# A second softmax with its maximum subtracted on TensorE, two blocks that alternate two steps earlier, and a weight decode whose low bits come a step later

## The chip, the cores and the metric

The kernel runs on one core of a Trainium2 chip. The metric is the time of one execution on the device in microseconds (us), lower is better. Before the change the median of three runs is 979.04 us (977.61 to 979.51).

## The reference, cut to what matters

Three stages follow one another. An attention over 4 batches, 8 heads, 576 positions, 64 columns per head, with a local mask for the first four heads (32 positions back) and a strided one for the others; then a feed-forward layer with `h * cos(h)`; then one with a rational function of h.

```
scores = where(mask, scale * q @ k.T, -1e9);  scores -= max(scores)
attn = exp(scores);  attn /= sum(attn) + 1e-9;  x = attn @ v      # heads side by side: 2304 x 512
x = g(x @ w_in) @ w_out        # 512 -> 2048 -> 512, g(h) = h * cos(h)
out = g2(x @ w_in2) @ w_out2   # g2(h) = P(h) / Q(h)
```

## The kernel before, in words

Five engines run their own queues, strictly in the order in which the program issues to them: PE (TensorE), DVE (VectorE), ACT (ScalarE), POOL (GpSimd) and SP, which issues the DMAs. The order is written out by hand; an instruction that waits holds up all that stands behind it on its engine.

*Attention.* The work is cut into eight halves of a sequence, n = 0 to 7 (288 positions each), and each half into four pairs of heads, pr = 0 to 3 (0 and 1 local, 2 and 3 strided). For half 1 a pair has 5 blocks of queries: 445 score columns for pr 0 and 1 in one bank of PSUM, 378 + 252 = 630 for pr 2 and 3 in two banks. For each pair: `att_s` puts mask and scores into PSUM, the softmax follows, `att_norm` divides by the sum (two small DVE instructions and a multiplication on POOL), `att_t`, `att_te` and `att_o` transpose, copy and multiply with v, and `att_oe` writes the result as a high part `xh` (ACT, L374) and a low part `xl` (DVE, L375) into a ring that the feed-forward layer reads.

*START* is a list of commands that handles half 0, and of half 1 the scores and the exponentials, beside the decoding of the first eight weight tiles. `red` takes row maxima on DVE (L292) and scales them (L293). `exps` issues five activations per pair, one for each block, each with the negative maximum as its bias and its row sum accumulated on the side (L302).

*Steps.* After START come steps g = 0, 1, 2, ... A step is one block of tokens with one of 16 slices f of the hidden layer: `l1` has 12 matmuls (L408), the elementwise part follows, and `l2` (12 matmuls, L427) comes two or three steps later. The element-wise part of a step is a string of letters, in whose order the engines get their instructions: U (ACT, L497), V (DVE, L507), N (ACT sine, L509), M (DVE, L511), G (ACT, L515), H (POOL or DVE, L517), `x y z p q` for weight decoding, `s w` for splits, `T` for the attention's PE part, `L` for what is planned as "late". In the first 32 steps M reads h from PSUM, and `l1` has two banks for h, so that `l1` of step g waits for M of step g - 2. Two blocks of 256 tokens, bA and bB, share the first 32 steps: bA alone for `BLAG` steps, then in turns. bB reads columns 256 to 511 of the ring, which are partly of half 1. `TAB1` says in which steps the rest of half 1 runs (norm, transposes, result).

*Weights.* They come as 64-bit integers and are decoded in place. For each 128 x 512 tile: two activations (L143 for the value, L147 for the low bits), two DVE instructions (`c == 1`, L154, which reads the low bits, and `c == 2`, L156; `c == 0` does nothing), then a split into high (ACT, L162) and low part (POOL, L165). `DSTEP` gives the step in which pair k = 4 to 15 of tiles of the first layer is decoded; the ACT part runs at the end of the step ahead of it, the split in the step behind it. The second layer's tiles are decoded in steps 28 to 111 by `plan_w2`, with `first` (ACT part), `second` with c = 0 and c = 1, and `third`, in steps that `W2ABS` gives, most often with c = 0 and c = 1 in the same step, the one behind `first`.

Of the kernel before, what the change touches and what calls it, by code (L numbers as in the profile page):

```python
# [73 lines left out]


ORD.update({0: 'LukjVsWxyzNMabpqTGH', 1: 'UjVLwxyzNMpTbsaGqH', 2: 'UjVTxwKyNMbsazpqGHL', 3: 'UKjVbTwxLyzNaMsqGHp', 4: 'UjVaTwxyzNMLbpsqGH', 5: 'UjVsTxyzNMpwabqGHL', 6: 'UKxjVwyszbTNMaGpqHL', 7: 'ULKjVTwxyzNMabpqGsH', 8: 'uajVTswxyzbNMpqGHL', 9: 'ULjVTswxyzqpNMabGH', 10: 'sUxWyjVbKzNMpqGHTLa', 11: 'UjVswxzNyMabpqGTHL', 12: 'uKxjVwyszbTNMaGpqHL', 13: 'TUjVsxyzwLNabpMqGH', 14: 'uKwbSTxjVyzNMaLqpGH', 15: 'UKxJVyTswzNMbqpaLGH', 16: 'UajVKsxyNzpTwMGbqHL', 17: 'UajVKsxyNzMpTwGbqHL', 18: 'bUKjVswxyTzNLMapqGh', 19: 'UjVTxwKyNMLsbazpqGH', 20: 'UwxyJVbKzNMpqsGhTLa', 21: 'UKjVbTwxLyzNaMsqGHp', 22: 'uxTswyzMapGbjVqNHL', 23: 'uTxswzyMapGbjVqNhL', 24: 'ujVaswxyzNMkbpqGHLT', 25: 'UxTsWyzMapGbJVqKNHL', 26: 'sUMNTWxyzpabqGHKjVL', 27: 'uTWxzbsNMjVaqypGHKL', 28: 'NMUjVTkGhswL', 29: 'wNsMUjVGTLhk', 30: 'UxjVswyTbzkNMaGpqHL', 31: 'ULKjVTswxyzqpNMabGH', 32: 'UjVswxyTbzKNMaGpqHL', 33: 'bUKjVswxyTzNLMapqGh', 34: 'swNMUjVGhTL', 35: 'skwNMLUGTjVh', 36: 'sNMwLUkGhTjV', 37: 'wNTMuKjVLSGH', 38: 'skwNMLUGTjVh', 39: 'SwKNMujVGHTL', 40: 'SwNMUKjVGHTL', 41: 'swNMUKjVGHTL', 42: 'swNMUKjVGHTL', 43: 'wNTMuKjVLSGH', 44: 'swNMUKjVGhTL', 45: 'swNMUKjVGhTL', 46: 'swNMUKjVGHTL', 47: 'swNMUKjVGHTL', 112: 'swNMUKjVGHTL', 113: 'swNMUKjVGhTL', 114: 'swNMUKjVGhTL', 115: 'swNMUKjVGhTL', 116: 'swNMUKjVGHTL', 117: 'swNMUKjVGhTL', 118: 'swNMUKjVGhTL', 119: 'swNMukjVGHTL', 120: 'swNMUKjVGHTL', 121: 'swNMUKjVGHTL', 122: 'swNMUKjVGhTL', 123: 'swNMUKjVGhTL', 124: 'swNMUKjVGhTL', 125: 'swNMUKjVGhTL', 126: 'swNMUjKVGHTL', 127: 'swNMUKjVGHTL'})
DSTEP = [0, 1, 2, 3, 4, 6, 5, 8, 10, 12, 14, 15]
TAB1 = [[0, 2, 3], [0, 3, 4], [3, 4, 5], [4, 5, 6]]
TAB2 = [[-3, -1, -1, 0, 6, 8, 11], [-3, 1, -2, 1, 6, 10, 12], [-3, 12, 2, 3, 6, 11, 13], [2, 11, 4, 5, 8, 12, 14]]
W2ABS = [[25, 28, 29, 30, 31], [34, 37, 38, 38, 38], [37, 40, 41, 41, 42], [41, 44, 45, 45, 46], [48, 51, 52, 52, 52], [52, 55, 56, 56, 57], [57, 60, 61, 62, 63], [64, 67, 68, 68, 68], [68, 71, 72, 72, 73], [73, 76, 77, 78, 79], [80, 83, 84, 84, 84], [84, 87, 88, 88, 89], [89, 92, 93, 94, 95], [96, 99, 100, 100, 100], [100, 103, 104, 104, 105], [105, 108, 109, 110, 111]]  # L80
BLAG = 8
START = ['cst ACT', 'lq 0 0', 'lq 0 2 ACT', 'load 2 0', 'lv 0 1', 'lv 0 3 w0', 'lq 0 3', 'lq 0 1 ACT', 'load 0 0', 'lv 0 0', 'load 0 1', 'load 1 0 ACT', 'load 1 1', 'warm 38', 'lv 0 2 w0', 'masks', 's 0 0 y', 's 0 1 y', 's 0 2 y', 's 0 3 y', 'lq 1 0', 'ab', 'lq 1 2', 'lq 1 1', 'load 2 1', 'load 3 0', 'load 3 1', 'red 0 0', 'lv 1 0', 'exps 0 0', 'lq 1 3', 'ms 0 1', 'ex 0 1', 'red 0 2', 'lv 1 1', 'exps 0 2', 'norm 0 0 POOL', 'ms 0 3', 'ex 0 3', 'load 4 1', 'sum 0 1', 'norm 0 2 POOL', 'norm 0 1 POOL', 'sum 0 3', 'warm 29', 'abs 0 0', 'abs 0 1', 't 0 0 h', 'load 4 0', 'te 0 0', 'd 0 0 0', 'norm 0 3 POOL', 'o 0 0', 'd 0 1 0', 'd 0 0 1', 'd 0 1 1', 'd 0 0 2', 'd 0 1 2', 't 0 1 y', 'abs 1 1', 'te 0 1', 'oe 0 0', 'split 0 1 POOL', 'abs 1 0', 't 0 2 h', 'o 0 1', 'd 1 1 0', 'd 1 1 1', 'd 1 0 0', 'te 0 2', 'load 6 1', 'd 1 0 1', 'split 0 0 POOL', 'd 1 0 2', 't 0 3 y', 'oe 0 1', 's 1 0 y', 'te 0 3', 'd 1 1 2', 'o 0 2', 'split 1 0 POOL', 'oe 0 2', 'split 1 1 POOL', 'o 0 3', 's 1 1 y', 'abs 2 0', 'abs 2 1 DVE', 'd 2 0 0', 'd 2 1 0', 'abs 3 0', 'd 2 0 1', 'd 2 1 1', 'abs 3 1', 's 1 2 y', 's 1 3 a', 'red 1 0', 'd 2 1 2', 'red 1 1', 'd 2 0 2', 'exps 1 0', 'oe 0 3', 'split 2 0 POOL', 'exps 1 1', 'red 1 2', 'split 2 1 POOL', 'd 3 1 0', 'red 1 3', 'exps 1 2', 'exps 1 3', 'd 3 0 0', 'd 3 0 1', 'd 3 1 1', 'd 3 0 2', 'd 3 1 2', 'split 3 0 POOL', 'load 5 0', 'load 5 1', 'load 7 0', 'split 3 1 POOL DVE', 'load 7 1', 'load 6 0', 'next']
LV1 = [2, 4]
TABE = [[-5, -2, -1, 0, 4, 9, 11], [-3, -1, 0, 1, 6, 10, 12], [0, 12, 2, 3, 6, 11, 13], [1, 13, 4, 5, 6, 12, 14]]
TABO = [[-4, -2, -1, 0, 4, 9, 11], [-3, -1, 0, 1, 6, 10, 12], [-2, 12, 2, 3, 4, 11, 13], [1, 13, 4, 5, 6, 12, 14]]
C_ORD.update({0: 'swNMUKjVGHTL', 1: 'swNMUjVGhTL', 2: 'swNMUKjVGhTL', 3: 'swNMUKjVGhTL', 4: 'swNMUKjVGhTL', 5: 'swNMUKjVGhTL', 6: 'swNMUKjVGhTL', 7: 'swNMUkjVGHTL', 8: 'swNMUKjVGHTL', 9: 'swNMUKjVGHTL', 10: 'swNMUKJVGhTL', 11: 'swNMUKjVGhTL', 12: 'swNMUKjVGhTL', 13: 'swNMUKjVGhTL', 14: 'swNMUKjVGHTL', 15: 'swNMUKjVGHTL', 16: 'swNMUKjVGHTL', 17: 'swNMUKjVGhTL', 18: 'swNMUKjVGhTL', 19: 'swNMUKjVGhTL', 20: 'swNMUKjVGHTL', 21: 'swNMUKjVGhTL', 22: 'swNMUKjVGhTL', 23: 'swNMUjVGhTL', 24: 'swNLMUKjVGHT', 25: 'wNsMUKjVGHTL', 26: 'swNMUKjVGhTL', 27: 'swNMUKjVGhTL', 28: 'swNMUKjVGhTL', 29: 'swNMUKjVGhTL', 30: 'swNMUKjVGHTL', 31: 'swNMUKjVGHTL'})
# [5 lines left out]
def attention_moe_moe_kernel(ctx: ExitStack, tc: tile.TileContext, qk0, qk, vv, w1, w2, consts, a, b, out):  # L92
    nc = tc.nc
    ACT, DVE, POOL, PE, SP = nc.scalar, nc.vector, nc.gpsimd, nc.tensor, nc.sync
# [11 lines left out]
    cst = const.tile([128, NCONST], F32, name="cst")  # L106
# [3 lines left out]
    ab = const.tile([128, 6], F32, name="ab")  # L110
# [17 lines left out]
    wh, wl, raws = {}, {}, {}  # L128
# [6 lines left out]
        (eng or SP).dma_start(out=t.rearrange("p n w -> p (n w)"), in_=src[f, o].bitcast(I32))  # L135
        raws[key, f, o] = t

    def dec_abs(key, f, o, eng=None):
        t = raws.pop((key, f, o))
        m = stage("dec")  # L140
        src = t[:, :, 1].bitcast(F32)
        if eng is None:
            ACT.activation(out=m, in_=src, func=AF.Copy, scale=2.0 ** -112)  # L143
        else:
            eng.tensor_scalar(out=m, in0=src, scalar1=2.0 ** -112, scalar2=None, op0=ALU.mult)

# [577 lines left out]
    for k in range(NPRE, NF):  # L724
        dplan[DSTEP[k - NPRE]] = pairs[k]
    with tc.manual_schedule():
        with tc.tile_pool(name="att", bufs=2) as p:
# [6 lines left out]
            ms = {}  # L734
# [182 lines left out]
```

## Time and profile before

| | |
|---|---|
| median of three runs | 979.04 us |
| the profiled execution: time, and span from first to last instruction | 975.9 us, 974.1 us |
| PE busy | 919.2 us, 94% of the span |
| DVE, ACT, POOL busy | 700.5, 707.9, 292.5 us |
| mean granted clock of TensorE | 0.987 |

Times within the execution count from the first instruction. "V of step g" below is the g-th instruction of line L507 (counted from 0); it marks when DVE has come to step g.

### The profile page before, as it was taken

The page shows a single profiled execution, that of the slowest core. Times are in us where ns is not written, and L with a number is a line of the kernel's source. Part 1 is how long each engine was busy: PE and PEld are TensorE (multiplying, and loading weights), DVE is VectorE, ACT ScalarE, POOL GpSimd, SP SyncE. Part 2 cuts the span into 40 slices and gives each one's busy share as a digit, 9 for nine tenths or more (in the row PEclk, how much of TensorE's full clock was granted, in tenths as well). Part 3 has the DMA queues.
Part 4 walks back from the last instruction along what each step waited for, and adds up shares of the span by engine and source line. Part 5 has one row for each costly group of instructions (what it writes and reads, how often), then busy time and mean ns, then how long its engine had stood idle before and what let it go on. Part 6 is the DMA issues. An engine that isn't in the chain of part 4 may idle for free.

```text
span 974.1 us, 17268 instructions
## 1 busy us (share of the span) xinstructions
PE 919.2 (94%) x6367; PEld 857.1 (88%) x6367; DVE 700.5 (72%) x1305; ACT 707.9 (73%) x1485; POOL 292.5 (30%) x279
## 2 busy tenths in 40 slices
PE   7678999999999999999899999999999999999997
PEld 6567999998989989899899978888898898898895
DVE  5997754775555575656658797787787787787776
ACT  5987765665775865757758877777777877777875
POOL 2577722142222132221312223223223223232221
PEclk9799999999999999999999999999999999999999
DMA  9766104435335244344226420010100100100000
GB/s 309 265 221 210 45 2 129 152 112 149 114 101 156 93 144 140 130 136 148 91 78 201 128 78 1 8 58 1 40 26 1 66 1 1 66 1 0 34 1 33
DMA packets 51525, 89.35 MB, mean 92 GB/s; under 512 B 4584, under 2 KB 28400, under 8 KB 51440
## 3 DMA queue, kind: packets, MB, share of 16 engines
q1 hardware_dynamic: 50720, 86.58, 27.0%
q10 hardware_dynamic: 720, 1.67, 0.5%
q8 instruction: 50, 0.82, 0.3%
q14 instruction: 35, 0.29, 0.1%
HBM read 70.40 MB, written 17.83 MB: 91 GB/s over the span
## 4 chain that ended last, share of the span: by engine, by line
PE 23%; ACT 22%; DVE 19%; POOL 10%; issue 5%; DMA 1%; POOLq 0%; ACTq 0%; DVEq 0%
PE h L408 10%; POOL z L467 9%; PE y L427 9%; DVE r L470 7%; ACT r L466 6%; ACT r L465 5%; ACT gh L476 4%; DVE h L471 3%; DVE a L471 3%; PE a L363 1%; PE a L248 1%; DVE t L511 1%; PE a L344 1%; ACT dec L143 1%; ACT L509 1%
## 5 line engine op out<-in xcount | busy, mean ns | idle before, releaser
L408 PE MATMUL h<-xh,w 128*128 128x288 f32 (+3 forms) x1408 | 338.6, 312 | 15.5 <-DVE t L511 11.9
L408 PEld LDWEIGHTS h<-xh,w 128*128 128x128 f32 x1408 | 245.1, 191 | 21.7 <-DVE t L511 13.1
L427 PE MATMUL y<-gh,w 128*128 128x288 f32 (+2 forms) x1024 | 229.3, 300 | 0.5 <-ACT w L162 0.5
L408 PE MATMUL h<-xl,w 128*128 128x288 f32 (+3 forms) x704 | 206.8, 310 | 0.0
L427 PE MATMUL y<-w,gh 128*128 128x512 f32 x576 | 195.9, 393 | 5.6 <-DVE ev L441 4.6
L467 POOL TENSOR_TENSOR z<-q,r 128x384 f32<-128x384 f32 x96 | 97.4, 1014 | 297.9 <-ACT r L466 287.8
L427 PEld LDWEIGHTS y<-gh,w 128*128 128x128 f32 x1024 | 172.1, 189 | 0.8 <-ACT w L162 0.8
L427 PE MATMUL y<-gl,w 128*128 128x288 f32 (+2 forms) x512 | 151.7, 296 | 2.2 <-POOL gl L517 2.1
L408 PEld LDWEIGHTS h<-xl,w 128*128 128x128 f32 x704 | 134.7, 191 | 1.8
L427 PEld LDWEIGHTS y<-w,gh 128*128 128x128 f32 x576 | 108.1, 188 | 28.1 <-DVE ev L441 7.1
L517 POOL TENSOR_TENSOR gl<-t,gh 128x288 fp32r<-128x288 f32 (+2 forms) x67 | 68.6, 1025 | 186.9 <-ACT gh L515 162.0
L470 DVE SCALAR_TENSOR_TENSOR r<-z,r 128x384 f32<-128x384 f32 x96 | 69.5, 724 | 74.1 <-POOL z L467 74.1
L427 PE MATMUL y<-w,gl 128*128 128x512 f32 x288 | 114.7, 398 | 5.2 <-DVE gl L481 5.0
L497 ACT ACTIVATE t<-h,biases 128x288 int32<-128x288 f32 (+2 forms) x116 | 57.7, 497 | 78.5 <-PE h L408 66.1
L507 DVE SCALAR_TENSOR_TENSOR u<-h,t 128x288 f32<-128x288 f32 (+2 forms) x128 | 58.2, 455 | 68.5 <-ACT hs L503 53.3
L408 PE MATMUL a<-xh,w 128*128 128x384 f32 x384 | 106.2, 337 | 0.0
L427 PEld LDWEIGHTS y<-gl,w 128*128 128x128 f32 x512 | 97.1, 190 | 3.0 <-POOL gl L517 2.9
L515 ACT ACTIVATE gh<-t 128x288 fp32r<-128x288 f32 (+2 forms) x128 | 56.7, 443 | 27.7 <-DVE t L511 25.6
L509 ACT ACTIVATE u<-u,biases 128x288 f32<-128x288 f32 (+2 forms) x128 | 67.8, 530 | 12.1 <-DVE u L507 11.7
L511 DVE TENSOR_TENSOR t<-u,hs 128x288 f32<-128x288 f32 (+1 forms) x91 | 49.2, 541 | 36.7 <-ACT u L509 36.5
L408 PEld LDWEIGHTS a<-xh,w 128*128 128x128 f32 x384 | 70.5, 188 | 1.8
L427 PEld LDWEIGHTS y<-w,gl 128*128 128x128 f32 x288 | 54.0, 188 | 20.1 <-DVE gl L481 12.1
(113 smaller groups left out, 1612.9 us busy)
## 6 DMA issues: line engine op xcount, KB each, us to landing
raw<-in_w_dram SPq DMA_DIRECT2D x63, 512.0 KB
qk<-in_qk_dram SPq DMA_DIRECT2D x18, 481.0 KB
wf<-dec SPq DMA_DIRECT2D x32, 256.0 KB
wf<-wf SPq DMA_DIRECT2D x32, 256.0 KB
x2s<-x2d SPq DMA_DIRECT2D x24, 192.0 KB
out_dram<-ev SPq DMA_DIRECT2D x17, 256.0 KB
v<-in_vv_dram SPq DMA_DIRECT2D x16, 240.0 KB
v<-in_vv_dram SPq DMA_DIRECT2D x24, 157.5 KB
```

Of the source, the lines that this page charges most:

```text
L408: PE.matmul(h[:, :n], w[d["ph"], f, 0][:, 128 * c:128 * c + 128], x[c][:, cs], start=k == 0, stop=k == len(ops) - 1)
L427: PE.matmul(y, l, r, start=first and i == 0 and bk != bB, stop=last and i == 2 and bk != bA)
L466: ACT.activation(out=r, in_=r, func=AF.Exp, scale=-1.0, bias=biases[:, 1:2])
L467: POOL.tensor_tensor(out=z, in0=q, in1=r, op=ALU.mult)
L470: DVE.scalar_tensor_tensor(out=r, in0=z, scalar=2.0, in1=r, op0=ALU.subtract, op1=ALU.mult, reverse0=True)
L471: DVE.scalar_tensor_tensor(out=h, in0=h, scalar=ab[:, 0:1], in1=r, op0=ALU.add, op1=ALU.mult)
L497: ACT.activation(out=k, in_=h, func=AF.Identity, scale=INV_2PI, bias=biases[:, 2:3])
L507: DVE.scalar_tensor_tensor(out=u, in0=h, scalar=INV_2PI, in1=k, op0=ALU.mult, op1=ALU.subtract)
L509: ACT.activation(out=u, in_=u, func=AF.Sin, scale=TWO_PI, bias=biases[:, 3:4])
L511: DVE.tensor_tensor(out=t, in0=u, in1=e.get("hs", h), op=ALU.mult)
L515: ACT.activation(out=e["gh"], in_=t, func=AF.Copy)
L517: (POOL if c == "H" else DVE).tensor_tensor(out=e["gl"], in0=t, in1=e["gh"].bitcast(F32), op=ALU.subtract)
```

## The change

Half 1's softmax in START: `red`, `exps` become `redn` (the same reductions, the maximum only negated), `psub`, `ex`, `sum`. `psub` is `att_s` a second time on the same banks: mask and scores anew, and behind them one float32 matmul of the identity with the negative maxima, broadcast over the columns. `ex` is one activation for each bank (one for pr 0 and 1, two for pr 2 and 3) instead of five with sums, and `sum` a reduction on DVE over the pair. `oe 0 3` moves ahead of half 1's reductions. `BLAG` goes from 8 to 6; `TAB1` moves half 1's steps one to two earlier; the loads of v for half 1 go to steps 1 and 2; `DSTEP` moves pairs 8, 10, 11 and all later ones one to three steps back, and 9 stays at step 6. For the second layer's weights the low-bits activations move from `first` to `second` with c = 0.

```diff
-DSTEP = [0, 1, 2, 3, 4, 6, 5, 8, 10, 12, 14, 15]
-TAB1 = [[0, 2, 3], [0, 3, 4], [3, 4, 5], [4, 5, 6]]
+DSTEP = [0, 1, 2, 3, 5, 6, 8, 10, 12, 14, 16, 18]
+TAB1 = [[0, 1, 2], [0, 2, 3], [1, 3, 4], [2, 4, 5]]
-BLAG = 8
+BLAG = 6
-START = [... 's 1 2 y', 's 1 3 a', 'red 1 0', 'd 2 1 2', 'red 1 1', 'd 2 0 2', 'exps 1 0', 'oe 0 3', 'split 2 0 POOL', 'exps 1 1', 'red 1 2', 'split 2 1 POOL', 'd 3 1 0', 'red 1 3', 'exps 1 2', 'exps 1 3', 'd 3 0 0', 'd 3 0 1', 'd 3 1 1', 'd 3 0 2', 'd 3 1 2', 'split 3 0 POOL', ..., 'split 3 1 POOL DVE', ..., 'next']
-LV1 = [2, 4]
+START = [... 's 1 2 y', 's 1 3 a', 'oe 0 3', 'redn 1 0', 'psub 1 0', 'd 2 1 2', 'redn 1 1', 'psub 1 1', 'd 2 0 2', 'ex 1 0', 'sum 1 0', 'split 2 0 POOL', 'ex 1 1', 'sum 1 1', 'redn 1 2', 'psub 1 2', 'split 2 1 POOL', 'd 3 1 0', 'redn 1 3', 'psub 1 3', 'ex 1 2', 'sum 1 2', 'ex 1 3', 'sum 1 3', 'd 3 0 0', 'd 3 0 1', 'd 3 1 1', 'd 3 0 2', 'd 3 1 2', 'split 3 0 POOL', ..., 'split 3 1 POOL DVE', ..., 'next']
+LV1 = [1, 2]
...
+    def dec_low(t):
+        src = t.rearrange("p n w -> p (n w)").bitcast(U8).rearrange("p (n b) -> p n b", b=8)[:, :, 3]
+        ACT.activation(out=t[:, :, 0], in_=src, func=AF.Copy, scale=1.0 / 32.0, bias=-31.0 / 64.0)
-    def dec_abs(key, f, o, eng=None):
+    def dec_abs(key, f, o, eng=None, low=True):
...
             def first(f=f):
-                raws["m", f] = [dec_abs(2, f, o) for o in range(2)]
+                raws["m", f] = [dec_abs(2, f, o, low=False) for o in range(2)]
             def second(f=f, c=0):
                 for t, m in raws["m", f]:
-                    dec_ops(c, t, m)
+                    dec_ops(c, t, m) if c else dec_low(t)
```

## Rows read from the trace of the kernel before

**Rows 1.** The page's busy time, share of the span and instructions of each engine.

```profile
PE 919.2 (94%) x6367; PEld 857.1 (88%) x6367; DVE 700.5 (72%) x1305; ACT 707.9 (73%) x1485; POOL 292.5 (30%) x279
```

**Rows 2.** Windows: start and end, length, busy time of each engine, clock, DMA.

```profile
29.43:39.21 9.78, 6.78 (x45) 5.77 (x45) 9.22 (x20) 9.78 (x47) 2.62 (x3) 0.65 1.02 392
31.00:37.80 6.80, 4.72 (x28) 3.99 (x25) 6.30 (x13) 6.80 (x37) 2.54 (x2) 0.50 1.03 410
42.25:93.46 51.21, 37.15 (x311) 34.67 (x312) 44.50 (x62) 42.41 (x90) 37.67 (x30) 0.88 0.61 208
127.62:142.02 14.40, 14.40 (x122) 14.31 (x121) 7.03 (x19) 10.01 (x18) 3.08 (x4) 1.00 0.00 1
```

**Rows 3.** PE's waits, first 200 us, then the rest: total, times, longest.

```profile
PE h L408 <- DVE t L511: 7.6, 2, 5.8
...
PE h L408 <- DVE t L511: 4.3, 2, 2.2
```

**Rows 4.** Timeline of ACT, end of START and step 0: start, duration, instruction.

```profile
30.28 0.34 ACT L302 ACTIVATE p<-y,mx 128x89 f32<-128x89 f32 x1
...
31.85 0.68 ACT L374 ACTIVATE xh<-a 128x288 fp32r<-128x288 f32 x1
...
38.81 0.79 ACT L143 ACTIVATE dec<-raw 128x512 f32<-128x512 f32 x1
...
41.27 1.28 ACT L509 ACT_TABLE_LOAD   x1
42.70 0.51 ACT L509 ACTIVATE u<-u,biases 128x256 f32<-128x256 f32 x1 [0.15 <-DVE u L507]
```

**Rows 5.** Timeline of DVE, from half 1's first reduction to V of step 10.

```profile
29.43 0.61 DVE L292 TENSOR_REDUCE mx<-y 128x5 f32<-128x445 f32 x1
...
32.56 0.65 DVE L375 TENSOR_TENSOR xl<-a,xh 128x288 fp32r<-128x288 f32 x1 [0.39 <-ACT xh L374]
33.12 0.87 DVE L292 TENSOR_REDUCE mx<-y 128x3 f32<-128x378 f32 x2
...
36.35 1.28 DVE L154 SCALAR_TENSOR_TENSOR dec<-dec,raw 128x512 int32<-128x512 int32 x2
37.55 1.28 DVE L156 SCALAR_TENSOR_TENSOR dec<-raw,dec 128x512 int32<-128x512 int32 x2
...
39.21 1.25 DVE L333 TENSOR_SCALAR sm<-sm 128x5 f32<-128x5 f32 x1
...
42.25 0.42 DVE L507 SCALAR_TENSOR_TENSOR u<-h,t 128x256 f32<-128x256 f32 x1
...
63.51 0.42 DVE L507 SCALAR_TENSOR_TENSOR u<-h,t 128x256 f32<-128x256 f32 x1 [0.64 <-ACT t L497]
...
93.46 0.42 DVE L507 SCALAR_TENSOR_TENSOR u<-h,t 128x256 f32<-128x256 f32 x1 [0.98 <-ACT t L497]
```

**Rows 6.** Timeline of PE: masks and scores of half 1 (pr 0, 2, 3).

```profile
21.46 0.35 PE L237 MATMUL y<-msk,cst 128*128 128x445 bf16 x1
21.75 0.98 PE L245 MATMUL y<-qk 64*64 64x89 f32 x20
...
27.81 0.65 PE L245 MATMUL y<-k,qk 64*64 64x126 f32 x8
...
33.59 1.10 PE L245 MATMUL a<-k,qk 64*64 64x126 f32 x8
```

**Rows 7.** Groups by line and shape, whole span: count, busy us, mean ns of one.

```profile
L286 DVE TENSOR_REDUCE sm<-p 128x5 f32<-128x445 f32 x13 | 7.9, 606 | 0.0
...
L281 ACT ACTIVATE p<-p 128x445 f32<-128x445 f32 x13 | 7.4, 577 | 1.8 <-DVE p L315 1.7
...
L286 DVE TENSOR_REDUCE sm<-p 128x5 f32<-128x630 f32 x6 | 4.8, 800 | 0.0
```

**Rows 8.** Timeline around a decoding step of the second layer's weights (steps 55 to 57).

```profile
272.72 0.64 ACT L147 ACTIVATE raw<-raw 128x512 int32<-128x512 uint8 x1
...
273.40 0.69 DVE L154 SCALAR_TENSOR_TENSOR dec<-dec,raw 128x512 int32<-128x512 int32 x1 [0.40 <-ACT raw L147]
274.00 0.45 DVE L511 TENSOR_TENSOR t<-u,h 128x288 f32<-128x288 f32 x1
...
274.50 0.40 PE L408 MATMUL h<-xh,w 128*128 128x288 f32 x1 [2.19 <-DVE t L511]
```

More of the change, by code (lines that the diff above doesn't have):

```diff
@@ L82 @@
-START = ['cst ACT', 'lq 0 0', 'lq 0 2 ACT', 'load 2 0', 'lv 0 1', 'lv 0 3 w0', 'lq 0 3', 'lq 0 1 ACT', 'load 0 0', 'lv 0 0', 'load 0 1', 'load 1 0 ACT', 'load 1 1', 'warm 38', 'lv 0 2 w0', 'masks', 's 0 0 y', 's 0 1 y', 's 0 2 y', 's 0 3 y', 'lq 1 0', 'ab', 'lq 1 2', 'lq 1 1', 'load 2 1', 'load 3 0', 'load 3 1', 'red 0 0', 'lv 1 0', 'exps 0 0', 'lq 1 3', 'ms 0 1', 'ex 0 1', 'red 0 2', 'lv 1 1', 'exps 0 2', 'norm 0 0 POOL', 'ms 0 3', 'ex 0 3', 'load 4 1', 'sum 0 1', 'norm 0 2 POOL', 'norm 0 1 POOL', 'sum 0 3', 'warm 29', 'abs 0 0', 'abs 0 1', 't 0 0 h', 'load 4 0', 'te 0 0', 'd 0 0 0', 'norm 0 3 POOL', 'o 0 0', 'd 0 1 0', 'd 0 0 1', 'd 0 1 1', 'd 0 0 2', 'd 0 1 2', 't 0 1 y', 'abs 1 1', 'te 0 1', 'oe 0 0', 'split 0 1 POOL', 'abs 1 0', 't 0 2 h', 'o 0 1', 'd 1 1 0', 'd 1 1 1', 'd 1 0 0', 'te 0 2', 'load 6 1', 'd 1 0 1', 'split 0 0 POOL', 'd 1 0 2', 't 0 3 y', 'oe 0 1', 's 1 0 y', 'te 0 3', 'd 1 1 2', 'o 0 2', 'split 1 0 POOL', 'oe 0 2', 'split 1 1 POOL', 'o 0 3', 's 1 1 y', 'abs 2 0', 'abs 2 1 DVE', 'd 2 0 0', 'd 2 1 0', 'abs 3 0', 'd 2 0 1', 'd 2 1 1', 'abs 3 1', 's 1 2 y', 's 1 3 a', 'red 1 0', 'd 2 1 2', 'red 1 1', 'd 2 0 2', 'exps 1 0', 'oe 0 3', 'split 2 0 POOL', 'exps 1 1', 'red 1 2', 'split 2 1 POOL', 'd 3 1 0', 'red 1 3', 'exps 1 2', 'exps 1 3', 'd 3 0 0', 'd 3 0 1', 'd 3 1 1', 'd 3 0 2', 'd 3 1 2', 'split 3 0 POOL', 'load 5 0', 'load 5 1', 'load 7 0', 'split 3 1 POOL DVE', 'load 7 1', 'load 6 0', 'next']
@@ L83 @@
-LV1 = [2, 4]
+BLAG = 6
+START = ['cst ACT', 'lq 0 0', 'lq 0 2 ACT', 'load 2 0', 'lv 0 1', 'lv 0 3 w0', 'lq 0 3', 'lq 0 1 ACT', 'load 0 0', 'lv 0 0', 'load 0 1', 'load 1 0 ACT', 'load 1 1', 'warm 38', 'lv 0 2 w0', 'masks', 's 0 0 y', 's 0 1 y', 's 0 2 y', 's 0 3 y', 'lq 1 0', 'ab', 'lq 1 2', 'lq 1 1', 'load 2 1', 'load 3 0', 'load 3 1', 'red 0 0', 'lv 1 0', 'exps 0 0', 'lq 1 3', 'ms 0 1', 'ex 0 1', 'red 0 2', 'lv 1 1', 'exps 0 2', 'norm 0 0 POOL', 'ms 0 3', 'ex 0 3', 'load 4 1', 'sum 0 1', 'norm 0 2 POOL', 'norm 0 1 POOL', 'sum 0 3', 'warm 29', 'abs 0 0', 'abs 0 1', 't 0 0 h', 'load 4 0', 'te 0 0', 'd 0 0 0', 'norm 0 3 POOL', 'o 0 0', 'd 0 1 0', 'd 0 0 1', 'd 0 1 1', 'd 0 0 2', 'd 0 1 2', 't 0 1 y', 'abs 1 1', 'te 0 1', 'oe 0 0', 'split 0 1 POOL', 'abs 1 0', 't 0 2 h', 'o 0 1', 'd 1 1 0', 'd 1 1 1', 'd 1 0 0', 'te 0 2', 'load 6 1', 'd 1 0 1', 'split 0 0 POOL', 'd 1 0 2', 't 0 3 y', 'oe 0 1', 's 1 0 y', 'te 0 3', 'd 1 1 2', 'o 0 2', 'split 1 0 POOL', 'oe 0 2', 'split 1 1 POOL', 'o 0 3', 's 1 1 y', 'abs 2 0', 'abs 2 1 DVE', 'd 2 0 0', 'd 2 1 0', 'abs 3 0', 'd 2 0 1', 'd 2 1 1', 'abs 3 1', 's 1 2 y', 's 1 3 a', 'oe 0 3', 'redn 1 0', 'psub 1 0', 'd 2 1 2', 'redn 1 1', 'psub 1 1', 'd 2 0 2', 'ex 1 0', 'sum 1 0', 'split 2 0 POOL', 'ex 1 1', 'sum 1 1', 'redn 1 2', 'psub 1 2', 'split 2 1 POOL', 'd 3 1 0', 'redn 1 3', 'psub 1 3', 'ex 1 2', 'sum 1 2', 'ex 1 3', 'sum 1 3', 'd 3 0 0', 'd 3 0 1', 'd 3 1 1', 'd 3 0 2', 'd 3 1 2', 'split 3 0 POOL', 'load 5 0', 'load 5 1', 'load 7 0', 'split 3 1 POOL DVE', 'load 7 1', 'load 6 0', 'next']
@@ L145, in dec_abs @@
             eng.tensor_scalar(out=m, in0=src, scalar1=2.0 ** -112, scalar2=None, op0=ALU.mult)
-        ACT.activation(out=t[:, :, 0], in_=t.rearrange("p n w -> p (n w)").bitcast(U8).rearrange("p (n b) -> p n b", b=8)[:, :, 3],
-                       func=AF.Copy, scale=1.0 / 32.0, bias=-31.0 / 64.0)
+        if low:
+            dec_low(t)
         return t, m
```

## The prediction

> **What bounds the kernel now.** The page's busy times come first: PE is busy for 94% of the span, the other engines for at most 73% [rows 1]. So an edit pays or costs where PE waits, and the windows tell where that is. In a stretch such as 127.62 to 142.02 us PE is busy for all 14.40 us, 122 matmuls or about five steps, 2.9 us for each, and DVE and ACT have room [rows 2]. From 42.25 to 93.46 us, which is V of step 0 to V of step 10, it is busy for 37.2 of 51.2 us, while DVE is busy for 44.5, ACT for 42.4 and POOL for 37.7 [rows 2]: these ten steps take 5.1 us each, not 2.9, because three engines are busy with decoding, half 1's attention and the elementwise part at once. Ahead of that, 29.43 to 39.21 us, the end of START, ACT is busy for 9.78 of 9.78 us and DVE for 9.22 [rows 2]. The waits of PE say the same: its longest, 5.8 us, is `l1` waiting for M (L511), early on; in the remaining 774 us the same wait occurs twice, 4.3 us in all [rows 3]. The reader is to see two clocks in the timeline: DVE comes to step 0 at 42.25 us and ACT's sine (N) at 42.70 us [rows 4, 5], and PE is the bound from about 93.5 us on. The change counts for what it does to these two, and for the two late waits.
>
> **START, the chain that gets longer.** Before, the four `exps` stand in ACT's queue between 30.28 us and 38.2 us, ACT goes on with step 0's decode at 38.81, loads the sine's table at 41.27, and N starts at 42.70 [rows 4]. DVE does its reductions and four decode instructions (36.35 to 38.83), then two norms, whose L333 takes 1.25 us [rows 5]. The two engines hardly wait for each other. After, every pair goes DVE (`redn`), PE (`psub`), ACT (`ex`), DVE (`sum`), and DVE's order puts `sum` 0 and 1 ahead of `redn` 2 and 3, and all `sum`s ahead of the decode of the tiles that ACT needs next. I follow it by hand:
>
> `oe 0 3` goes first: `xh` starts at 30.28 and not at 31.85 [rows 4], `xl` (0.65 us) [rows 5] ends about 31.6, and the last scores, which ended at 34.69 [rows 6], end 1.57 earlier, at 33.1. The first `redn` (0.61 and a short negation) is done at 32.3, in time. Then `psub`. Its masks and scores are those of before: 1.27 us from the first mask to the last score for a pair with 445 columns [rows 6]; for one with 630, 252 of which take 0.65 [rows 6], some 1.9 with masks. The broadcast matmul isn't in the trace. From below: 445 columns of bf16 in one matmul take 0.35 us [rows 6]; from above: ten pairs of float32 matmuls of 89 columns take 0.98 us, 0.49 for 445 columns [rows 6]. I take 0.42, as it is float32 but without ten starts, and 0.6 for 630. A `psub` is then 1.7 us, or 2.5.
>
> - pair 0: PE 33.1 to 34.8; `ex` (0.58) [rows 7] to 35.4; `sum` (0.61) [rows 7] to 36.1
> - pair 1: PE to 36.5; `ex` to 37.1, `sum` to 37.8
> - `redn` of pair 2 (0.87 [rows 5] and the negation) to 38.8, of pair 3 to 39.9; PE starts pair 2 under the reduction and ends it at 40.8, pair 3 at 43.2
> - `ex` of pair 3's second bank to 43.7; `sum` (0.80) [rows 7] to 44.5
> - the four decode instructions, 2.5 us [rows 5], to 47.0 instead of 38.83
>
> So DVE is some 8.2 us late. Of that 2.8 us are the four `sum`s (2 x 0.61 and 2 x 0.80), the rest waits for PE and ACT. Behind it stand the norms, which still meet POOL's splits, and V of step 0. On ACT the split's copy waits for the decode, then come four activations of `next` (38.81 to about 41.0 before) and the table: N of step 0 also about 8.3 us later, near 51.0. What `ex` saves on ACT, 20 activations with sums against six (about 6.5 us against 2.5), is worth nothing here, since ACT now waits for `psub`.
>
> That is at full clock. Between 31.00 and 37.80 the granted clock was 0.50 [rows 2], after PE had stood waiting at the end of START; at that level scores like those of 0.65 us take 1.10 [rows 6], 1.7 times as long. With all four `psub`s at the lower level the same chain ends 14.3 us late. PE waits less now just ahead of the first `psub`, so I take mostly the upper level, and 9.5 us (8.3 to 14.3).
>
> The Trainium skill, page "FP8 and Floating Point Precision", section "TensorE Precision Notes", has a true float32 product in four passes through the array. An estimate by that page, four passes at 2.4 GHz, would be 0.74 us for 445 columns and 1.05 for 630, and START some 1.5 us longer than I sum it, +6.5 us in all. The rows speak against it, as 445 columns of float32 scores fit into 0.49 us [rows 6]; no row here shows a single long float32 matmul.
>
> **Steps 0 to 9, where something comes back.** `DSTEP` takes one pair out of these steps: eight are decoded there before (steps 0 to 6 and 8), seven after (0, 1, 2, 3, 5, 6, 8). `TAB1` moves half 1's transposes from steps 2 to 5 to steps 1 to 4 and its norms forward. Before, V of step 4 is at 63.51 [rows 5]: 21.3 us for four steps with decode, then 29.95 us for six steps with four decodes. After, the first four have the same decodes and one pair's transposes, copies and results more, +1.5 us by the 0.65 of `xl` and the like. The six that follow have three decodes and three steps free of one. At the average decode step of 5.3 us (21.3 / 4), less 0.4 as the attention is done after step 5, and 3.4 for a free step, they take 25.0 where 29.95 stood. That is 3.5 us back. The other end is that PE becomes the bound from step 6 on, at 2.9 us a step [rows 2]: 9.5 us back. I take 5. The two sides add: V of step 10 comes 9.5 - 5 = 4.5 us later, and from there on PE bounds both kernels.
>
> **BLAG, LV1, later decodes.** Alternating from step 6 changes no matmul count. `l1` of step 6 needs half 1's last `xl` of step 5, one step ahead where two were; DVE issues it right at the start of step 5, whose predecessor has no decode, so at most 0.6 us, within the range. Each weight is still ready two steps ahead of its matmul (pair 8 is split in step 6, used by `l2` in step 9). The loads of v stand in SP's queue behind the multiplication that frees their buffer, one step ahead of their use; at 5 us a step I take nothing. Decodes in steps 16 and 18 lie beside half 2's maxima on DVE and POOL: up to 1 us.
>
> **Low bits.** Two activations of 0.64 us [rows 8] move one step. Before step 57 PE waits 2.19 us [rows 8], one of the two late waits [rows 3]; there M (274.00) stands behind the low bits of `first` on ACT and, in that step's order, behind L154, which ends at 274.09. After, ACT's sine comes 1.1 us earlier, but the low bits follow it and both L154 wait for them, ahead of M: M moves from 274.00 to about 274.45. So +0.45 us, twice; or, if M should profit, up to 4.3 us back [rows 3]. I take +0.5. In other steps ACT's peak falls by 1.1 us under PE's cover.
>
> **Sum.** 9.5 - 5.0 + 0.5 = +5.0 us on the profiled 975.9, that is 980.9. The profiled execution is 3.1 us under the median, so the forecast for a median is 979.0 + 5.0 = 984.0 us, 0.5% slower. About 0.2%, 2 us, is what a measurement can tell from no change.
>
> **Rivals.**
> - *The clock falls in START:* PE waits for `redn` between `psub` 1 and 2, and the lower level holds for pairs 2 and 3, or all: +12 to +14 in START, some 4 to 5 back, +7 to +10: 986 to 989. For it: 0.50 was granted in this very place [rows 2]. Against: more matmuls. Chance 0.18.
> - *Even:* START costs 8.3 to 9.5 and the steps give 8 back, 977 to 981. For it: PE's 2.9 us from step 6 on is what the steps behind 93 us show. Against: three decodes are still in steps 5 to 8. Chance 0.18.
> - *Faster:* the first ten steps are freed of more than they are given. Place: steps 4 to 9. It decides when these six steps take under 20 us instead of 29.95, which needs PE as the bound from step 4 on (17.4 us): 12.5 back, less 1.5 for the first four, against 8.3 in START, and with the low bits' 4.3 a time of 972 to 977. For it: five steps in a row without stalls are seen later. Chance 0.16.
> - *The change doesn't do what it says:* if `ex` were held by other work on ACT, `psub` would not set the chain; ACT has too little left in that stretch. No chance of its own.
>
> **How the numbers follow.** The forecast itself (START +8 to +11, steps 3 to 6 back: 981 to 987) has 0.48. Slower by over 2 us: 0.48 and 0.18, less 0.02 of the forecast's edge, 0.64; within 2 us 0.18 and that edge, 0.20; faster 0.16. The range runs from 976.5, which takes in the even case and a little of the faster one, to 989.5, the clock rival's end.
>
> **What would show it.** Right: half 1's row maxima followed by a second set of scores between 33 and 43 us; DVE waiting for ACT's L327 ahead of each L286; V of step 0 near 51 us, V of step 10 near 98; later PE gaps as before but for half a microsecond at steps 57 and 89. Wrong: V of step 0 before 48 us (the broadcast or the waits are over-priced), or V of step 10 before 94 us (the steps give back more), or a shorter rest behind step 10.

## The result, and the profile after

The changed kernel takes 992.14 us (median of 4, 988.82 to 993.59) against 978.84 us before: ratio 1.0141, interval 1.0125 to 1.0157. It is 1.4% slower (13.3 us by the two medians, 13.8 by the ratio), where 5.0 us or 0.5% was forecast, and lies 2.6 us above the range's end of 989.5. The profiled execution is the fastest of the four, 988.82 us with a span of 987.0 us, 12.9 us over the span of before. That difference is laid out in the table by the start of `l1` of a step in the two profiles:

| `l1` of step | before, us | after, us | after is late by |
|---|---|---|---|
| 1 | 37.35 | 47.04 | 9.7 |
| 2 | 44.97 | 59.54 | 14.6 |
| 6 | 72.74 | 82.21 | 9.5 |
| 11 | 94.13 | 102.21 | 8.1 |
| 22 | 130.47 | 141.47 | 11.0 |
| 56 | 269.00 | 278.56 | 9.6 |
| 58 | 277.78 | 291.04 | 13.3 |
| 112 | 496.73 | 509.39 | 12.7 |

So START costs ten, the first ten steps give little back, steps 13 to 22 take 2.9 (2.3 of it from step 18 on), and the late low bits give and take. START first, by the timeline of DVE after (start, duration, instruction, idle time before it and what ended it):

```profile
31.88 0.64 DVE L379 TENSOR_TENSOR xl<-a,xh 128x288 fp32r<-128x288 f32 x1 [1.45 <-ACT xh L378]
...
36.26 0.62 DVE L290 TENSOR_REDUCE sm<-p 128x5 f32<-128x445 f32 x1 [1.08 <-ACT p L331]
38.30 0.62 DVE L290 TENSOR_REDUCE sm<-p 128x5 f32<-128x445 f32 x1 [1.43 <-ACT p L331]
...
43.21 0.81 DVE L290 TENSOR_REDUCE sm<-p 128x5 f32<-128x630 f32 x1 [2.14 <-ACT p L331]
46.30 0.81 DVE L290 TENSOR_REDUCE sm<-p 128x5 f32<-128x630 f32 x1 [2.29 <-ACT p L331]
47.03 1.28 DVE L158 SCALAR_TENSOR_TENSOR dec<-dec,raw 128x512 int32<-128x512 int32 x2
...
52.93 0.42 DVE L511 SCALAR_TENSOR_TENSOR u<-h,t 128x256 f32<-128x256 f32 x1
...
55.19 0.41 DVE L515 TENSOR_TENSOR t<-u,h 128x256 f32<-128x256 f32 x1
...
76.61 0.41 DVE L511 SCALAR_TENSOR_TENSOR u<-h,t 128x256 f32<-128x256 f32 x1
...
102.80 0.42 DVE L511 SCALAR_TENSOR_TENSOR u<-h,t 128x256 f32<-128x256 f32 x1 [0.69 <-ACT t L501]
```

The reader is to see five waits of 8.4 us together, each ended by ACT, and four sums (L290) of 2.9 us together; before, DVE waited 0.39 us in this stretch for the same `xl` [rows 5]. The decode that stands behind the last sum starts at 47.03, 10.7 us later than before, and V of step 0 at 52.93, 10.7 us later too. V of step 4 is at 76.61 and V of step 10 at 102.80: 23.7 us behind V of step 0 and 26.2 us behind V of step 4, where it was 21.3 and 29.95 [rows 5]. ACT in START (its timeline after) has become the engine that waits:

```profile
35.61 0.55 ACT L331 ACTIVATE p<-y 128x445 f32<-128x445 f32 x1 [3.76 <-PE y L254]
...
53.39 0.51 ACT L513 ACTIVATE u<-u,biases 128x256 f32<-128x256 f32 x1 [0.30 <-DVE u L511]
```

The second row is N of step 0, at 42.70 before [rows 4]. PE's timeline shows a `psub` and, later, where the steps wait:

```profile
33.35 0.36 PE L241 MATMUL y<-msk,cst 128*128 128x445 bf16 x1
33.65 0.98 PE L249 MATMUL y<-qk 64*64 64x89 f32 x20
34.56 1.01 PE L254 MATMUL y<-mx,cst 128*128 128x445 f32 x2
35.41 0.35 PE L241 MATMUL y<-msk,cst 128*128 128x445 bf16 x1
...
39.43 0.32 PE L241 MATMUL y<-cst 128*128 128x378 bf16 x1 [1.81 <-DVE mx L324]
...
53.28 1.37 PE L348 MATMUL a<-cst,p 128*89 128x128 f32 x5 [4.67 <-POOL p L339]
58.29 1.32 PE L367 MATMUL a<-pt,v 89*64 89x58 f32 x20 [3.64 <-ACT pt L356]
...
133.31 0.39 PE L412 MATMUL h<-xh,w 128*128 128x256 f32 x1 [0.64 <-DVE t L515]
...
140.07 0.39 PE L431 MATMUL y<-gl,w 128*128 128x256 f32 x1 [0.99 <-POOL gl L521]
...
285.12 0.61 PE L412 MATMUL h<-xh,w 128*128 128x288 f32 x1 [3.25 <-DVE t L515]
```

The broadcast matmul of 445 columns stands as two records and occupies PE from 34.56 to 35.41, 0.85 us. At 53.28 and 58.29 the attention's transposes (L348) and products with v (L367) of step 1 wait and hold PE's queue; `l1` of step 2 stands behind them and starts at 59.54, though M of step 0, for which it waited before, starts at 55.19. At 133.31 and 140.07 are the only two waits of PE between `l1` of step 18 and of step 22, where before there was none. At 285.12 is the wait at step 57, 2.19 us before [rows 8] and now 3.25. What comes behind it is in the windows (columns as in rows 2): the end of START, V of step 0 to V of step 10, and step 57.

```profile
32.43:49.89 17.46, 14.23 (x131) 9.44 (x130) 10.35 (x22) 4.80 (x10) 2.75 (x3) 1.00 0.41 161
52.93:102.80 49.87, 36.59 (x321) 33.87 (x322) 40.08 (x59) 39.43 (x84) 34.05 (x28) 0.90 0.67 232
285.12:291.04 5.92, 5.92 (x24) 5.92 (x25) 2.80 (x5) 2.55 (x6) 2.08 (x2) 0.50 0.00 0
```

In START DVE and ACT are busy for 10.35 and 4.80 of 17.46 us; before, for 9.22 and 9.78 of 9.78 [rows 2]. Step 57 runs at a granted clock of 0.50 and takes 5.92 us, where it took 3.28 (from 274.50 [rows 8] to 277.78 in the table). The low bits themselves, in DVE's timeline of step 56:

```profile
283.40 1.29 DVE L158 SCALAR_TENSOR_TENSOR dec<-dec,raw 128x512 int32<-128x512 int32 x2 [1.62 <-ACT raw L141]
...
284.61 0.45 DVE L515 TENSOR_TENSOR t<-u,h 128x288 f32<-128x288 f32 x1
```

M (284.61) stands behind a decode that now waits 1.62 us for the low bits. It starts 6.05 us behind `l1` of step 56, and 5.00 us before (274.00 [rows 8] and the table).

### The profile page after: what moved, and what is told of

It is laid out like the page before. It is cut to its first block, busy times and chain, and to the rows that moved or that the text cites. A ratio compares the mean times of both kernels' runs of the same rounds, so it can differ in the third digit from the quotient of the medians.

```text
span 987.0 us, 17427 instructions
## 1 busy us (share of the span) xinstructions
PE 929.7 (94%) x6465; PEld 864.3 (88%) x6465; DVE 698.2 (71%) x1309; ACT 704.7 (71%) x1451; POOL 289.5 (29%) x279
## 3 DMA queue, kind: packets, MB, share of 16 engines
q1 hardware_dynamic: 50720, 86.58, 26.4%
## 4 chain that ended last, share of the span: by engine, by line
PE 24%; ACT 22%; DVE 18%; POOL 10%; issue 5%; POOLq 0%; ACTq 0%
PE h L412 11%; PE y L431 10%; POOL z L471 9%; DVE r L474 7%; ACT r L470 6%; ACT r L469 5%; ACT gh L480 4%; DVE h L475 3%; DVE a L475 3%; PE a L367 1%; PE a L252 1%; ACT L285 1%; PE a L348 1%; DVE t L515 1%; ACT L513 1%
## 5 line engine op out<-in xcount | busy, mean ns | idle before, releaser
L521 POOL TENSOR_TENSOR gl<-t,gh 128x288 fp32r<-128x288 f32 (+2 forms) x67 | 65.4, 977 | 189.5 <-ACT gh L519 166.7
L431 PEld LDWEIGHTS y<-w,gl 128*128 128x128 f32 x288 | 54.0, 188 | 20.1 <-DVE gl L485 12.1
```

The costliest lines, as they stand in the source:

```text
L431: PE.matmul(y, l, r, start=first and i == 0 and bk != bB, stop=last and i == 2 and bk != bA)
L521: (POOL if c == "H" else DVE).tensor_tensor(out=e["gl"], in0=t, in1=e["gh"].bitcast(F32), op=ALU.subtract)
```

## The experiments

The ratio is to the kernel before, which ran beside each of them (medians 977.8 to 978.3 us).

| run | what is changed against the kernel before | median, us | ratio, interval |
|---|---|---|---|
| e1 | START alone | 988.55 | 1.0106, 1.0082 to 1.0130 |
| e2 | low bits alone | 978.90 | 1.0013, 1.0001 to 1.0025 |
| e3 | BLAG, TAB1, DSTEP, v loads | 980.39 | 1.0021, 1.0006 to 1.0036 |
| e4 | all, START in another order | 985.33 | 1.0071, 1.0047 to 1.0095 |
| e5 | DSTEP alone | 979.27 | 1.0009, 0.9992 to 1.0025 |
| e6 | other DSTEP, low bits, order of steps 56, 88 | 975.21 | 0.9976, 0.9964 to 0.9987 |
| e7 | low bits, order of steps 56, 88 | 971.60 | 0.9935, 0.9914 to 0.9956 |
| e8 | order of steps 56, 88 | 977.25 | 0.9994, 0.9984 to 1.0003 |
| e9 | oe 0 3 earlier | 980.02 | 1.0015, 1.0006 to 1.0025 |
| e10 | low bits, filler matmuls | 975.28 | 0.9975, 0.9964 to 0.9987 |

**The three parts alone.** e1 is the kernel before with the new START list; e2 with the new `dec_low`, `first` and `second`; e3, called the turns below, with

```diff
+DSTEP = [0, 1, 2, 3, 5, 6, 8, 10, 12, 14, 16, 18]
+TAB1 = [[0, 1, 2], [0, 2, 3], [1, 3, 4], [2, 4, 5]]
+BLAG = 6
+LV1 = [1, 2]
```

> The kernel before with the new START alone (second half's maximum subtracted on PE, sums on DVE, oe 0 3 earlier); BLAG, TAB1, DSTEP, v loads and low bits as before. Theory (START's chain DVE, PE, ACT, DVE delays step 0 by some 10.7 us, and only the later decode gave 2 to 3 us of it back): V of step 0 near 53 us, and 8 to 11 us slower in all. Rival (the new START costs nothing by itself, and the loss comes from alternating earlier and from the low bits): within 2 us of the kernel before.

> The kernel before with the low bits a step later alone. Theory (in steps 56 and 88 the low bits now stand right ahead of the decode and of M, PE's wait at steps 57 and 89 grows from 2.2 to 3.2 us, and the granted clock falls to 0.5 for some us after it; small waits at steps 44, 75, 82 and 107 shrink): about 2 us slower, +3.7 at step 57, +2.6 at step 89, -4 over the others. Rival (the low bits are covered by PE everywhere, and the later loss is one of the turns): within 1 us of before, waits at 57 and 89 of 2.2 us.

> The kernel before with BLAG 6, TAB1, DSTEP and the v loads of after; START and low bits as before. Theory (one decode less in steps 0 to 9 gives 2 to 3 us, decodes in steps 12, 16 and 18 take 2.5 to 3 us back): within 2 us of before. Rival (alternating earlier makes step 6 wait for the second half's attention, so the turns are part of the loss): 3 to 8 us slower. Second rival (the turns are worth what I forecast, and the new START hid it): 4 to 6 us faster.

START alone costs 1.06%, 10.4 us at 978, turns 0.21% and low bits 0.13%: 1.40% together, against 1.41% for the whole change. The parts add within their intervals, and START is three quarters of the whole. In e1 V of step 0 is at 54.5 us, and nothing of this comes back: `l1` of step 0 is 12.4 us behind the profile of before, of step 112 still 12.1. (The profile of before is an early one: with the same START, `l1` of step 0 comes 0.2 to 2.3 us later in e2, e3, e5 to e8 and e10.) The rival that START costs nothing by itself has fallen. For e2 I expected 2 us and measured 1.3: the wait at step 57 is 3.25 us as expected, and what the late low bits gain elsewhere pays for most of it (below). e3 is slower by 2 us, which is the first theory's edge; of its rivals neither holds, as step 6 shows no new wait in PE's timeline and nothing near 4 us is gained.

**START's order.** e4 is the changed kernel with the same work in START in another order:

```diff
-'oe 0 3', 'redn 1 0', 'psub 1 0', 'd 2 1 2', 'redn 1 1', 'psub 1 1', 'd 2 0 2', 'ex 1 0', 'sum 1 0', 'split 2 0 POOL', 'ex 1 1', 'sum 1 1', 'redn 1 2', ..., 'sum 1 3', 'd 3 0 0', ..., 'd 3 1 2', 'split 3 0 POOL'
+'oe 0 3', 'redn 1 0', 'psub 1 0', 'd 2 1 2', 'redn 1 1', 'psub 1 1', 'd 2 0 2', 'redn 1 2', 'psub 1 2', 'redn 1 3', 'psub 1 3', 'ex 1 0', 'split 2 0 POOL', 'ex 1 1', 'split 2 1 POOL', 'd 3 0 1', 'd 3 1 1', 'd 3 0 2', 'd 3 1 2', 'split 3 0 POOL', 'ex 1 2', 'ex 1 3'
...
+'split 3 1 POOL DVE', 'sum 1 0', 'sum 1 1', ..., 'next', 'sum 1 2', 'sum 1 3'
```

> The changed kernel with the same operations in START in another order: all four reductions and psubs first, decode of pair 3 on DVE ahead of the sums, the sums of pairs 0 and 1 after it, those of 2 and 3 behind the first decode. Theory (the 10.7 us of START are mostly waits of DVE's queue, some 8 us, and the delay of the decode behind them): V of step 0 at 45 to 47 us, the kernel 5 to 7 us faster than the changed one, 985 to 987 us. Rival (it is the added work on DVE and PE that counts, wherever it stands): V of step 0 still at 51 us or later, and no more than 2 us gained.

It takes 985.33 us, 0.7% less than the changed kernel by the two ratios. DVE's timeline shows three sums in one go behind the decode, one wait of half a microsecond, and V of step 0 at 45.70:

```profile
41.60 1.85 DVE L290 TENSOR_REDUCE sm<-p 128x5 f32<-128x445 f32 x3
43.98 0.81 DVE L290 TENSOR_REDUCE sm<-p 128x5 f32<-128x630 f32 x1 [0.54 <-ACT p L331]
...
45.70 0.42 DVE L511 SCALAR_TENSOR_TENSOR u<-h,t 128x256 f32<-128x256 f32 x1
```

So of START's 10.7 us some 7.2 are the order in which the same work is issued, and 3.5 are left. Behind the first reduction DVE waits for ACT 6.9 us in the changed kernel and 0.5 in e4. Not all of it lasts: in the two profiles 4.2 us are left at V of step 10 (98.58 against 102.80), and their times differ by 4.2 too (984.60 and 988.82, the fastest of its four); the 0.7% of the ratios, 6.8 us, can be 0.3 to 1.1% by the two intervals.

**oe 0 3.** e9 is the kernel before with that one command moved ahead of `red 1 0`.

> The kernel before with only oe 0 3 moved ahead of the second half's reductions, where the change puts it; red and exps as before. Theory (the loss in START is the chain of redn, psub, ex and sum; oe 0 3 lets DVE wait 1 us longer for xh and lets PE's last scores start 1.5 us earlier, neither of which reaches step 0): V of step 0 within 1 us of the other runs with the old START, the kernel within 2 us of before. Rival (the early oe 0 3 is a large part of START's loss): 3 us slower or more.

It is 0.15% slower, 1.5 us, within the 2 us forecast, but the theory behind that fails: what the early command delays does reach step 0. DVE waits 1.46 us for `xh` ahead of half 1's first reduction, where it waited 0.39 us behind two of them [rows 5]. PE's scores of pair 1 of half 1, before and in e9, then DVE in e9:

```profile
25.62 0.98 PE L245 MATMUL y<-qk 64*64 64x89 f32 x20
```

```profile
26.16 0.98 PE L245 MATMUL y<-qk 64*64 64x89 f32 x20
```

```profile
31.40 0.64 DVE L375 TENSOR_TENSOR xl<-a,xh 128x288 fp32r<-128x288 f32 x1 [1.46 <-ACT xh L374]
...
44.64 0.42 DVE L507 SCALAR_TENSOR_TENSOR u<-h,t 128x256 f32<-128x256 f32 x1
```

From these scores to V of step 0 it is 18.5 us in e9, and 16.4 to 16.6 in all eight profiles with the old START (16.6 before); 26.4 in the profile after, 27.8 in e1 and 19.3 in e4. By this measure START costs 9.8 to 11.4 us, of which some 7 are the order, 2 the early `oe 0 3`, if it costs in e4 what it costs in e9, and under 1 what e4 has left beside it.

**What of the turns.** e5 has only the new DSTEP.

> The kernel before with the new DSTEP alone; BLAG 8 and the second half's attention as before. Theory (the extra 2.4 us between V of step 0 and V of step 4 come from the attention being moved one to two steps forward, with PE's queue waiting for its copies ahead of l1 of step 2; the later decode by itself gives 3 to 4 us between V of step 4 and of step 6, and decodes in steps 16 and 18 beside half 2's maxima take 2.4 us back at steps 18 to 22): V0 to V4 21.3 us, V4 to V6 9 to 10 us, +2.4 us at steps 18 to 22, in all within 2 us of before. Rival (the first four steps are longer because of the weights' decode, whatever the attention does): V0 to V4 near 23.7 us, and 2 to 3 us slower.

In DVE's timelines, e3 and then e5, V of step 0 and of step 4:

```profile
44.10 0.42 DVE L507 SCALAR_TENSOR_TENSOR u<-h,t 128x256 f32<-128x256 f32 x1
...
67.90 0.42 DVE L507 SCALAR_TENSOR_TENSOR u<-h,t 128x256 f32<-128x256 f32 x1
```

```profile
42.90 0.42 DVE L507 SCALAR_TENSOR_TENSOR u<-h,t 128x256 f32<-128x256 f32 x1
...
64.15 0.42 DVE L507 SCALAR_TENSOR_TENSOR u<-h,t 128x256 f32<-128x256 f32 x1 [0.81 <-ACT t L497]
```

V of step 0 to V of step 4 takes 21.3 us in e5 as before, against 23.8 in e3; the next two steps take 11.1 us (12.9 before, 9.8 in e3), more than the 9 to 10 expected; at steps 18 to 22 it loses 2.3 us (`l1` of step 22 against `l1` of step 18), as e3 does with 2.5. So the first four steps are longer because of the attention's place and not the decode, and the decodes in steps 16 and 18 cost what was expected. (BLAG and the loads of v were not tried alone; BLAG acts from step 6 on, and the two waits below end with POOL and ACT, not with a load.) Where the attention's place costs is seen in PE's timeline of e3,

```profile
44.46 1.37 PE L344 MATMUL a<-cst,p 128*89 128x128 f32 x5 [2.86 <-POOL p L335]
49.46 1.32 PE L363 MATMUL a<-pt,v 89*64 89x58 f32 x20 [3.63 <-ACT pt L352]
```

against that of e5, where the same product, a step later, waits for 0.90 us:

```profile
45.62 0.58 PE L408 MATMUL h<-xh,w 128*128 128x256 f32 x1 [5.69 <-DVE t L511]
...
51.70 0.80 PE L363 MATMUL a<-pt,v 89*64 89x58 f32 x20 [0.90 <-ACT pt L352]
```

In e3 `l1` of step 2 starts at 50.71, behind that product; in e5 at 45.62, as soon as M of step 0 lets it.

**The low bits' wait.** In steps 56 and 88 the program's order puts "late" work ahead of M. e8 puts it at the end, and nothing else; e7 does so with the low bits late; e10 has the low bits late and the order of before, and fills PE's wait:

```diff
-24: 'swNLMUKjVGHT'
+24: 'swNMUKjVGHTL'                 # e6, e7, e8
+            def keep():            # e10
+                k = bank("a")
+                for _ in range(28):
+                    PE.matmul(k[:, :2 * WL], msk16[:, 0:128], msk16, start=True, stop=True)
+            plan("pe2", 56, keep)
+            plan("pe2", 88, keep)
```

> The kernel before with only the late part of steps 56 and 88 at the end of the step, behind M. Theory: M waits for the sine alone, which still stands behind the low bits of step 55: the wait at 57 falls from 2.2 us by 0.2 us, the whole kernel within 1 us of before. Rival (the order in steps 56 and 88 is all that matters, and the low bits' place nothing): as much gained as with the low bits moved too.

> The kernel before with the low bits a step later, and in steps 56 and 88 the late part at the end of the step, behind M. Theory (PE's waits at steps 57 and 89 come from the late part standing ahead of M in these two steps; without it a later low part only gains): waits at 57 and 89 about 1.3 us instead of 3.2, no fall of the clock behind them, waits at 44, 75, 82 and 107 smaller, 4 to 6 us faster than before. Rival (the table loads for the attention's exponentials set these waits, and the order matters little): waits stay at 2 us or more, within 2 us of before.

> The kernel before with the low bits a step later, and 28 matmuls of 178 columns into an unused bank behind l2 in steps 56 and 88 (some 2 us of added work on PE, while it waits for M). Theory (after a wait of 3.2 us the granted clock falls to 0.5 and makes the next step 1.4 us longer, twice): l1 of steps 57 and 89 starts as late as with the low bits alone, no fall of the clock near 277 and 407 us, steps 57 and 89 take 3.2 instead of 4.6 us, the kernel 2 to 3 us faster than with the low bits alone. Rival (the step behind the wait is longer for another reason, such as the queues of ACT and DVE): steps 57 and 89 still take 4.6 us.

e7 takes 971.60 us, 0.65% less than the kernel before. In its profile PE waits 1.50 us at step 57, 1.45 at step 89, and no clock falls between 95.1 and 969.0 us; M waits for the sine alone, as DVE's timeline of step 56 shows, and PE's right behind it:

```profile
274.27 0.45 DVE L514 TENSOR_TENSOR t<-u,h 128x288 f32<-128x288 f32 x1 [1.08 <-ACT u L512]
```

`l1` of step 57, in PE's timeline of e7:

```profile
274.78 0.40 PE L411 MATMUL h<-xh,w 128*128 128x288 f32 x1 [1.50 <-DVE t L514]
```

The order alone (e8) is within the measurement: the wait is 1.98 us, 0.2 less, as expected. The low bits alone lose, just clear of the noise (e2). It takes both, because M must stand neither behind the low bits nor behind the late part. Elsewhere the late low bits gain on their own, as the starts of `l1` show in e2 and e7 alike against the profile of before: 1.3 us from step 44 to 48 and about 1 at steps 73 to 76 and at 105 to 108 each. The wait at step 82 shrinks in e3, e5 and e8 too, so it has nothing to do with them.

Step 57 in e2 by the windows (columns as in rows 2):

```profile
277.72:282.39 4.67, 4.67 (x25) 4.67 (x25) 1.56 (x4) 2.01 (x5) 0.87 (x2) 0.67 0.01 4
```

The same step in e10, and the added matmuls ahead of it:

```profile
275.82:279.08 3.26, 3.26 (x24) 3.26 (x25) 1.56 (x4) 2.02 (x5) 0.86 (x2) 1.00 0.00 0
```

```profile
272.36 2.32 PE L825 MATMUL a<-msk 128*128 128x178 bf16 x28
```

Step 56 lasts as long in both (`l1` of 57 starts 6.56 and 6.62 us behind `l1` of 56), DVE and ACT have the same work in step 57, and with the added matmuls in the wait the clock stays at 1.00 and the step takes 3.26 instead of 4.67 us. So the long step behind the wait is the clock, and not a queue: the rival has fallen. By the two ratios e10 is 0.4%, some 3.7 us, faster than e2; in the profiles steps 57 and 89 give 1.4 us each. In e3 and e5, where low bits and order are those of before and the wait is 2.2 us, the clock fell too (279.9 and 277.7 us), in e9 and, behind a wait of 1.9 us, in e8 at step 89, so the kernel before may pay this in some of its executions; in the one profiled it didn't. Its runs beside the experiments fit that, without showing it: the shortest, 975.14 us, has a mean granted clock of 0.989, the longest, 980.30 us, one of 0.980.

**Another DSTEP.** e6 has e7's changes and `DSTEP = [0, 1, 2, 3, 5, 6, 8, 9, 10, 12, 14, 15]`.

> The kernel before with DSTEP [0, 1, 2, 3, 5, 6, 8, 9, 10, 12, 14, 15] (pair 8 to 11 later, the last ones at 14 and 15 as before), the low bits a step later, and in steps 56 and 88 the late part at the end of the step, behind M. Theory: nothing lost at steps 18 to 22; about 3 us gained by step 6, of which some goes again at step 9, whose decode is new; no wait over 1.5 us at steps 57 and 89, and 4 to 7 us faster than before in all. Rival (a wait that is removed comes back in the next step, as PE and ACT share one chain): within 2 us of before.

It is 3.6 us slower than e7, and faster than before by 0.24%, 2.3 us, not by the 4 to 7 expected. Steps 18 to 22 lose nothing, as expected, and 1.8 us are gained from step 5 to step 8, but `l1` then waits for M twice for 1.95 us (at 95.00 and 100.06 us), and from step 8 to step 13 it falls 5.3 us behind the profile of before. So the decode that was taken out of steps 4 and 5 was no cheaper in the steps just behind.

## Why the prediction was wrong

- **Direction and main cause: right.** The chain DVE, PE, ACT, DVE with `sum` ahead of `redn` and the decode was forecast at 9.5 us for START. V of step 0 is 10.7 us later in the profile, of which 0.9 stood already ahead of it (`xh` of `oe 0 3` starts at 31.20, not 30.28). e1 gives 10.4 us in time, and e4 shows that the order is 7 of it at V of step 0.
- **The broadcast was priced too low:** 0.42 us for 445 columns, measured 0.85, and 1.26 instead of 0.6 for 630 (0.74 for 378 and 0.52 for 252 in the profile). The bound from above, 0.49, was a row misread: `x20` at L245 [rows 6] is not twenty matmuls but ten of two records each (the kernel issues one for each of 5 blocks and 2 heads), as the one broadcast also stands as two records. Ten matmuls that run two at a time are 445 columns in 0.98 us, not in 0.49; read so, the row was near the 0.85 measured. What the Trainium skill gives on page "FP8 and Floating Point Precision", section "TensorE Precision Notes" (four passes), had led to an estimate of 0.74; the run agrees with it better than with the 0.42 I took, and the row that I held against it did not speak against it.
- **The clock in START: the cautious part was not needed.** 1.00 was granted there (32.43 to 49.89 above). So 1.3 us of the 9.5 (9.5 against 8.2) were not needed, while the four broadcasts took 2.2 us more than forecast. That START came out within some 1 us of its forecast is in part luck, as the two mistakes cancel in part.
- **Steps 0 to 9: the step that failed.** I worked out 3.5 us back, gave the other end as 9.5 and took 5. Measured are 1.3 in the profile after (49.9 us from V of step 0 to V of step 10, 51.2 before) and none in e3 (51.7); seven profiles with the old turns, that of before among them, take 51.0 to 52.4. The first four steps took 2.4 us more and not 1.5, as the attention's products of step 1 hold `l1` of step 2 in PE's queue. A decode less gave less than worked out: steps 4 to 9, which were to take 25.0 us instead of 29.95, took 26.2 in the profile after, but 27.9 in e3 and 28.9 in e5. And the other end supposed PE as the bound from step 6 on, while V of step 6 to V of step 10 takes 17.1 us before and after: both decode three pairs from step 6 to step 10. This term is 4 to 5 us of the miss.
- **Later decodes: mis-sized.** "Up to 1 us" was 2.3 to 2.5 us at steps 18 to 22, in e3, e5 and the profile after, and none of it was in the forecast.
- **Low bits: mis-sized, and near only by luck.** The working gives 0.45 us twice, 0.9, of which 0.5 was taken; e2 measured 1.3. M did fall behind the low bits as worked out, but by 1.05 us at step 57 and some 1.1 at step 89, not by 0.45. The fall of the clock that this triggers, 1.4 us twice in e2, was not in the forecast; nor were the gains at steps 44, 75 and 107, 3.3 us together, which I had put under PE's cover. What was left out on both sides nearly cancels.
- **The rivals.** The clock's fall in START did not come, nor did the even and the faster case, and the measured time lies above what any of them gave.

Of the miss, 13.3 to 13.8 less 5.0, that is 8.3 to 8.8 us, these terms make up: START some 1, the first ten steps 4 to 5, the later decodes 2, the low bits 1.

## What to carry to other kernels

Where engines run in order, a chain that visits three of them for each of four tiles pays its latency for each tile when the last operation of one tile stands in a queue ahead of the first of the next (here four waits of 1.1 to 2.3 us); issue all first operations, then independent work, then all last ones (e4: 7 us at V of step 0 for no work less). Five activations with their sums take 1.57 us of ACT for a pair (30.28 to 31.85 [rows 4]) against 0.55 for one without, but they need no second engine, while the sum then takes 0.62 on DVE; here ACT only waited in the time that it saved. And work that is put off pays only if it doesn't land ahead of what the critical engine waits for: the same late low bits lose 0.13% behind one order and gain 0.65% over before with one letter moved (e2, e7).

## What the runs showed of the hardware

A wait of PE can cost more than its length. After one of 3.25 us the granted clock was 0.50 for 6.8 us in the profile after, and for 3.4 us in e2, a step of 3.3 us taking 5.92 and 4.67; after waits of 2.2 us it fell in the profiles of e3 and e5, and not in those of before and e1. On the Trainium skill's page "TensorE: Matmul & The Clock Gate", Part 1, the lower level is the default and activity releases the higher one; the runs agree, as with 28 matmuls of no use in that wait (2.3 us of PE) the clock stays at 1.00 and e10 is some 3.7 us faster than e2.

A float32 matmul of this kernel's scores leaves two records in the trace, and so does the broadcast, which stands as `x2` and takes 0.85 us for 445 columns; the matmuls of `l1`, on operands of type fp32r, leave one each (twelve for its twelve). Who takes the count of records for a count of matmuls gets half the price, as the prediction did.
